# Sigmoid attention and a gated FFN on one core: two pairs of gate and value columns of the first group as block products

## The chip, the cores and the metric

One Trainium2 chip, of which the kernel uses one core. The time is the device time of one execution in microseconds; the figure for a kernel is the median of its runs. The engines of the core are PE (TensorE, matrix products), DVE (VectorE), ACT (ScalarE), POOL (GpSimd) and SP (SyncE, here only a queue that issues DMAs). Each runs its own instructions in the order in which the program lists them, and waits on semaphores for the others.

## The reference

```python
# q, k, v: (8, 12, 448, 64); w_gate, w_val: (768, 1536); w_out: (1536, 768); all float32
scores = scale * np.matmul(q, k.transpose(0, 1, 3, 2)) - np.log(S)      # scale = 1/sqrt(64), S = 448
attn = 1.0 / (1.0 + np.exp(-scores))                                    # a sigmoid, no softmax
attn_out = np.matmul(attn, v)
x = attn_out.transpose(0, 2, 1, 3).reshape(8 * 448, 12 * 64)            # 3584 tokens of 768
gate = np.maximum(x @ w_gate, 0.0)
val = x @ w_val
return gate * val @ w_out                                               # (3584, 768)
```

So eight batches each go through attention, and their 448 tokens each through a gated FFN whose weights are the same for all.

## The kernel before

The engine order is written out by hand (`tc.manual_schedule()`, L73): what the Python code calls first, each engine does first. Buffers come from pools; an instruction that writes a buffer waits until the earlier readers of it are done.

**Attention.** Twelve heads form six pairs, and two pairs make one of three head groups g. A unit (`qk_unit`, L294) is one key chunk c of seven for one g: 16 small matmuls in fours give the scores, two banks of PSUM, and two sigmoids on ACT write `PT`. When all seven chunks of a g are there, `pv_group` does 28 matmuls and DVE scales the two results into `xT` (L184). Each batch b has 21 units, cut into five or six steps m by the list `cuts`. k and q must be transposed first. For batches 0 and 1, PE does it (`pe_transposes`). From batch 2 on, DVE copies rows into `rel` (L215) and SP issues a DMA that transposes them into `qkT` (`dma_transposes`, L211).

**FFN, two ways.** Two batches make a group of 896 tokens. Plain (`gv`, L328): for one f of twelve (128 gate columns and the same value columns) six matmuls for the gate and six for the value; ACT takes the positive part, DVE multiplies into `hT`. In blocks (`gv_units`, L503): gate and value together, of both batches of a group, are a two by two block product which is done with seven products in place of eight (Strassen's scheme in Winograd's form). It needs sums of weights (`gate_sums`, `unit_sums`) and sums of `xT` blocks (`batch_sums`, which overwrites one block of `xT` in place), and it adds up with copies on ACT and DVE. One such unit does two f: seven products for each, three matmuls of 448 columns to a product. It uses six banks `b`, `a`, `c` (two each), and the seventh product adds into `b`, after DVE has read `b` in `plus` (L530). The down projection is done in the same way for pairs of 128-token tiles (`down_pair`, L429): seven products of six matmuls of 384 columns, with sums of `hT` blocks (`token_sums`, `more_token_sums`) and sums of `wo` (`weight_sums` 0 to 3, L397, once in the kernel, which need both halves of `wo`). Tile number 3 of an odd group takes the last 128 tokens of the group before it, which lie in `aside`.

**Which way where.** Group 0 (batches 0 and 1) goes the plain way for all twelve f, in `gv_queue`: each step of batches 1, 2 and 3 takes `mix[m]` of them from the queue after its units, and `hooks[m]` puts other work between them. Batch 0 is done in two halves of the queries (256 and 192 columns), so each f gives two entries for it and one for batch 1. Groups 1 to 3 go the block way: steps with `mix[m]` of 0 call `next_work`, which takes one entry of `work`: a pair of f, or a down pair. `jobs` run inside such an entry after its second product (`beside`), `behind` after its last.

**Loads.** All inputs and weights go through POOL's queue (`load`, `load_v`, `load_gv`, `load_o`), in the program's order and with fp32 turned to fp16 on the way. `hold` (L646) is a tiny copy on POOL that reads a transposed `qkT`; what stands behind it on POOL is issued only when that transpose has landed. The twelve f of `wg` and `wv` are all loaded before the last inputs of batch 1. `load_v(2)` follows `hold(2, 1)` at the end of batch 1 (L653). k, q and v of batch 3 follow in the first step of batch 2 (L759). `load_o(0)` and `load_o(1)` follow `hold(3, 1)` and `hold(3, 2)` in the fourth and sixth step of batch 2 (L716 to L718).

**Weight sums in batch 3.** `weight_sums(0)` is a hook of step 1, 1 and 2 one of step 2, and 3 a job of step 3, which is the first down pair.

Of the kernel before, what the change touches and what calls it, by code (L numbers as in the profile page):

```python
# [17 lines left out]
def kernel(  # L18
# [19 lines left out]
    NFC = DF // P  # L38
    TW = 2 * NCH
    QCUT = 4  # L40
    HALVES = ((0, QCUT), (QCUT, NCH))

    qk_scale = 1.0 / math.sqrt(D)
# [8 lines left out]
    relp = ctx.enter_context(tc.tile_pool(name="relp", bufs=2))  # L52
    qkTp = ctx.enter_context(tc.tile_pool(name="qkTp", bufs=3))
    PTp = ctx.enter_context(tc.tile_pool(name="PTp", bufs=11))
    xTp = ctx.enter_context(tc.tile_pool(name="xTp", bufs=3))
    hTp = ctx.enter_context(tc.tile_pool(name="hTp", bufs=1))
    ysbp = ctx.enter_context(tc.tile_pool(name="ysbp", bufs=4))
    gsbp = ctx.enter_context(tc.tile_pool(name="gsbp", bufs=6))
    first_sbuf = ExitStack()
    early = first_sbuf.enter_context(tc.tile_pool(name="early", bufs=1))  # L60
# [92 lines left out]
    load_gv(2, 4)  # L153
    load_gv(4, 6)
    load(1, 0, 1, "kq")
    load_gv(6, 9)
    load(1, 1, 2, "kq")
    load_gv(9, 12)
    load_v(1)
    load(1, 2, 3, "kq")  # L160

# [250 lines left out]
        sub(S2, S1, A11)  # L412
        sums["y"] = S1, S2, S4

    def more_token_sums(g, p):
        A11, A12, A21, A22 = token_blocks(g, p)
        S1, S2, S4 = sums["y"]
        sub(S4, A12, S2)
        sub(A21, A11, A21)

    def scaled(o, ps):
        nc.vector.tensor_scalar(
# [67 lines left out]
        lo, hi = slice(*ks), slice(HD + ks[0], HD + ks[1])  # L490
        return [late["X"][:, i, lo] for i in range(3)] + [x1[:, lo], x1[:, hi], x2[:, lo], x2[:, hi]]

    def batch_sums_t1(g):
        T1, _, _, B11, _, B12, _ = batch_blocks(g, (0, HD))
        sub(T1, B12, B11)

    def batch_sums(g, ks):
        T1, T2, T4, _, B21, B12, B22 = batch_blocks(g, ks)
        sub(T2, B22, T1)
        sub(B12, B22, B12)  # L500
        sub(T4, B21, T2)

    def gv_units(g, fs, beside, first_copy, then, split):  # L503
        x1, x2 = xT_tiles[2 * g], xT_tiles[2 * g + 1]
        T1, T2, T4 = (late["X"][:, i] for i in range(3))
        B11, B21, T3, B22 = x1[:, 0:HD], x1[:, HD:NDC], x2[:, 0:HD], x2[:, HD:NDC]
        b, a, c = ([bank(nm) for _ in fs] for nm in ("u", "g1", "g2"))
        later((4, 5, 6, 7, 2, 3))
        gs = [[gsbp.tile([P, S], FP32, tag="gsb", name="gsb") for _ in range(3)] for _ in fs]
        sets = []  # L510
        for u, f in enumerate(fs):
            us, cols = slice(u * P, (u + 1) * P), slice(f * P, (f + 1) * P)
            S1, S2, S4 = (t[:, :, us] for t in sums["w"])
            sets.append((
                wg[:, 0:HD, cols], wg[:, HD:NDC, cols], wv[:, HD:NDC, cols],
                S1, S2, wv[:, 0:HD, cols], S4,
            ))
        del sums["w"]

        def product(ps, i, W, first=True):  # L520
            for u in range(len(fs)):
                products([(ps[u], S, HD, sets[u][i], W, first)])

        def copy(i, ps, by=nc.scalar.copy):
            for u in range(len(fs)):
                by(gs[u][i][:], ps[u][:, 0:S])  # L526

        def plus(i, ps):
            for u in range(len(fs)):
                nc.vector.tensor_tensor(  # L530
                    out=gs[u][i][:], in0=ps[u][:, 0:S], in1=gs[u][i][:], op=AOP.add
                )

        product(b, 0, B11)
        copy(0, b, first_copy)
        product(a, 1, B21)
        beside()
        plus(0, a)
        product(b, 4, T2, False)
        copy(1, b)  # L540
        product(c, 3, T1)
        copy(2, c)
        product(b, 5, T3, False)
        plus(2, b)
        product(c, 6, B22, False)
        plus(1, c)
        product(b, 2, T4, False)

        def finish(even):
            for u in range(len(fs)):  # L550
                if even:
                    gated(g, fs[u], 0, S, gs[u][0], b[u])
                else:
                    gated(g, fs[u], S, S, gs[u][1], gs[u][2])

        if split:
            finish(False)
            then()
            finish(True)
        else:  # L560
            finish(True)
            finish(False)
            then()

    gv_queue = deque()

# [61 lines left out]
                after[(i, u)]()  # L628
    slots[5].pv()
    push_first(1, range(0, 6))  # L630
    for f0 in range(6, 12, 2):
        for half in range(2):
            push_first(half, range(f0, f0 + 2))

# [3 lines left out]
    def pv_finish(b):  # L638
        pv_group(b, NG - 1)
        if b < 2:  # L640
            push_gv(b, 0, S, range(NFC))

    first_psum.close()
    open_banks("ring1")
# [8 lines left out]
    def late_loads():  # L653
        dma_transposes(2, 1)
        hold(2, 1)
        load_v(2)


    work = deque()

    def push_group(g):
        if g > 0:
            work.extend([("w", g, (f, f + 1)) for f in range(0, NFC, 2)])
        work.extend([("y", g, p) for p in ((3, 0, 1, 2) if g % 2 else (0, 1, 2))])

    def prepare():
        if work:
# [6 lines left out]
    def next_work(jobs=(), behind=(), alone=False):  # L674
        kind, g, i = work.popleft()

        def run(jobs):
            for job in jobs:
                job()

        if kind == "y":
            down_pair(
                g, i, lambda: (more_token_sums(g, i), run(jobs)),
                lambda: (run(behind), prepare()), not work, scaled_act if alone else scaled,
            )
        else:
            first_copy = nc.scalar.copy if alone else nc.vector.tensor_copy
            if work[0][0] == "w":
                gv_units(g, i, lambda: (prepare(), run(jobs)), first_copy, lambda: run(behind), False)
            else:  # L690
                gv_units(
                    g, i, lambda: run(jobs), first_copy, lambda: (run(behind), prepare()), alone
                )

    ffn_mix(1, [(1, lambda: both(1, 0))])
    for b in range(1, B):
# [6 lines left out]
        count = len(cuts) - 1  # L703
        hooks = {}
        if b == 1:
            mix = (3, 3, 3, 3, 3, 2)
            hooks = {
                1: [(1, lambda: both(1, 1))],
                3: [(1, lambda: both(1, 2))],
                4: [(3, lambda: dma_transposes(2, 0))],  # L710
                5: [(2, late_loads)],
            }
        elif b == 2:
            mix = (2, 2, 1, 1, 2, 1)
            hooks = {
                3: [(0, lambda: (dma_transposes(3, 0), dma_transposes(3, 1), hold(3, 1), load_o(0)))],  # L716
                5: [
                    (1, lambda: (dma_transposes(3, 2), hold(3, 2), load_o(1))),  # L718
                    (0, lambda: (gate_sums(0, 2), gate_sums(2, 4))),
                ],  # L720
            }
            open_late()
        elif b == 3:
            mix = (1, 1, 1, 0, 0)
            hooks = {
                0: [(0, lambda: (gate_sums(4, 6), gate_sums(6, 8)))],
                1: [(0, lambda: weight_sums(0))],
                2: [(0, lambda: (prepare(), weight_sums(1), weight_sums(2)))],
            }
        else:  # L730
            mix = (0,) * count
        for m in range(count):
            jobs, behind = [], []
            for i, (g, c) in enumerate(order[cuts[m] : cuts[m + 1]]):
                if m in pv_at and i == pv_at[m][1]:
                    if m == 0:
                        pv_finish(b - 1)
                        if b == 2:
                            push_group(0)
                    else:  # L740
                        pv_group(b, pv_at[m][0])
                qk_unit(b, g, c)
            if m == 0 and b > 1 and b != 3:
                jobs.append(lambda: dma_transposes(b, 2))
            if b == 3 and m == count - 2:
                jobs.append(lambda: weight_sums(3))
            elif b == 4 and m == 2:
                jobs.append(lambda: (gate_sums(8, 10), gate_sums(10, 12)))
            elif b == 3 and m == count - 1:
                jobs.append(lambda: (dma_transposes(4, 0), dma_transposes(4, 1)))  # L750
            elif 0 <= m - count + 2 and 3 < b < B - 1:
                jobs.append(lambda: dma_transposes(b + 1, m - count + 2))
            if b == 1:
                if m == 0:
                    load(2, 0, 1, "kq")
                    load(2, 1, 2, "kq")
                    load(2, 2, 3, "kq")
            elif m == 0 and b + 1 < B:
                jobs.append(lambda: (load(b + 1, 0, 3, "kq"), load_v(b + 1)))  # L759
            if b % 2 and b > 2:  # L760
                if m == count - 1:
                    push_group(b // 2)
                    (jobs if b == B - 1 else behind).append(
                        lambda: (batch_sums_t1(b // 2), batch_sums(b // 2, (0, 1)))
                    )
                    if b == B - 1:
                        jobs.append(lambda: pv_finish(b))
                        behind.append(lambda: batch_sums(b // 2, (1, HD)))
            elif b > 3 and m == 0:
                behind.append(lambda: batch_sums(b // 2 - 1, (1, HD)))  # L770
            if mix[m]:
                for job in jobs:
                    job()
# [35 lines left out]
```

## Time and profile before

| | |
|---|---|
| runs | 404.38, 405.57, 405.37, 405.56, 404.32 us |
| median | 405.37 us |
| the profiled execution | 404.38 us, span of its instructions 402.6 us |
| mean granted PE clock | 0.993 |

The span runs from the first to the last instruction. Busy times of the engines overlap, so they don't add up to it. Where PE has a gap, what matters is what it waited for, and then why that was late. Two granted clocks below 1 show in the record: one stretch of 3.4 us between 113.99 and 117.40 us at half speed, and one at the very end.

| stage of the first half | from | to |
|---|---|---|
| batch 1, six steps | 33.84 | 62.98 |
| batch 2, six steps | 62.98 | 92.90 |
| batch 3, steps 0 to 2 | 92.90 | 105.81 |
| batch 3, step 3 (first down pair) | 105.81 | 119.78 |
| batch 3, step 4 (second down pair) | 119.78 | 130.94 |

These are the starts of the score matmuls in PE's timeline.

### The profile page before, as it was taken

The page shows a single profiled execution, that of the slowest core. Times are in us where ns is not written, and L with a number is a line of the kernel's source. Part 1 is how long each engine was busy: PE and PEld are TensorE (multiplying, and loading weights), DVE is VectorE, ACT ScalarE, POOL GpSimd, SP SyncE. Part 2 cuts the span into 40 slices and gives each one's busy share as a digit, 9 for nine tenths or more (in the row PEclk, how much of TensorE's full clock was granted, in tenths as well). Part 3 has the DMA queues.
Part 4 walks back from the last instruction along what each step waited for, and adds up shares of the span by engine and source line. Part 5 has one row for each costly group of instructions (what it writes and reads, how often), then busy time and mean ns, then how long its engine had stood idle before and what let it go on. Part 6 is the DMA issues. An engine that isn't in the chain of part 4 may idle for free.

```text
span 402.6 us, 8701 instructions
## 1 busy us (share of the span) xinstructions
PE 389.0 (97%) x3476; PEld 217.2 (54%) x3476; DVE 280.1 (70%) x570; ACT 230.0 (57%) x482; POOL 49.3 (12%) x74
## 2 busy tenths in 40 slices
PE   8999999999888999999999999999999999999995
PEld 3678775544444554554555555455455555555562
DVE  2453435344577799999766889999785699897661
ACT  5946777779815565655656565565545544433221
POOL 8643302301400300003000030000000000000000
PEclk9999999999989999999999999999999999999999
DMA  9999995998997794235916598012203220000235
GB/s 149 195 199 205 204 149 93 184 182 151 173 168 140 152 213 73 46 47 63 186 41 166 126 148 183 16 32 47 47 2 80 80 78 2 0 1 2 78 99 138
DMA packets 67257, 43.69 MB, mean 109 GB/s; under 512 B 35856, under 2 KB 63760, under 8 KB 67216
## 3 DMA queue, kind: packets, MB, share of 16 engines
q0 software_dynamic: 29200, 23.33, 37.9%
q1 hardware_dynamic: 37584, 19.24, 22.8%
q10 hardware_dynamic: 432, 0.56, 0.5%
q8 instruction: 27, 0.44, 0.4%
q14 instruction: 14, 0.11, 0.1%
HBM read 47.19 MB, written 11.01 MB: 145 GB/s over the span
## 4 chain that ended last, share of the span: by engine, by line
PE 86%; DMA 6%; DVE 3%; ACT 3%; issue 1%; ACTq 0%; POOL 0%; POOLq 0%
PE u L384 33%; PE g L384 15%; PE y L384 9%; PE qk_ps L232 7%; PE pv_ps L250 6%; PE g_ps L333 6%; PE v_ps L333 6%; DMA qkT<-rel 3%; DMA wo<-in_moe_w_out_dram 2%; ACT PT L187 2%; PE warm_ps L175 1%; PE trt L201 1%; DVE hT L319 1%; DVE xT L184 1%; ACT ysb L427 1%
## 5 line engine op out<-in xcount | busy, mean ns | idle before, releaser
L187 ACT ACTIVATE PT<-qk_ps 128x448 f16<-128x448 f32 (+3 forms) x318 | 150.8, 591 | 55.5 <-PE qk_ps L232 55.2
L384 PEld LDWEIGHTS <-S 128*128 128x128 f16 x576 | 56.4, 98 | 49.9 <-issue 4.7
L232 PE MATMUL qk_ps<-qkT 64*64 64x448 f16 (+2 forms) x756 | 50.2, 336 | 2.3 <-DMA qkT<-rel 1.5
L427 ACT ACTIVATE ysb<-u 128x384 f32<-128x384 f32 x32 | 15.7, 491 | 58.4 <-PE u L384 58.2
L526 ACT COPY gsb<-u 128x448 f32<-128x448 f32 x48 | 25.6, 533 | 31.8 <-PE u L384 30.5
L384 PEld LDWEIGHTS <-hT 128*128 128x128 f16 x312 | 30.0, 99 | 24.2 <-issue 3.1
L530 DVE TENSOR_TENSOR gsb<-g,gsb 128x448 f32<-128x448 f32 x72 | 41.5, 617 | 0.1
L319 DVE SCALAR_TENSOR_TENSOR hT<-gate_sb,v_ps 128x256 f16<-128x256 f32 (+2 forms) x36 | 14.6, 421 | 37.4 <-ACT gate_sb L342 21.1
L250 PE MATMUL pv_ps<-PT,v 64*64 64x448 f16 (+2 forms) x756 | 37.2, 329 | 0.7 <-issue 0.7
L184 DVE TENSOR_SCALAR xT<-pv_ps 128x448 f16<-128x448 f32 (+2 forms) x53 | 27.8, 566 | 14.1 <-PE pv_ps L250 13.5
L232 PEld LDWEIGHTS <-qkT 64*64 64x64 f16 x756 | 20.2, 105 | 26.9 <-issue 15.8
L333 PE MATMUL g_ps<-xT,wg 128*128 128x256 f16 (+2 forms) x216 | 33.5, 291 | 0.1
L333 PE MATMUL v_ps<-xT,wv 128*128 128x256 f16 (+2 forms) x216 | 33.3, 290 | 0.0
L384 PEld LDWEIGHTS <-wv 128*128 128x128 f16 x216 | 21.1, 98 | 19.7
L384 PEld LDWEIGHTS <-wg 128*128 128x128 f16 x216 | 20.3, 98 | 20.6 <-issue 3.0
L384 PE MATMUL u<-wo,hT 128*128 128x384 f16 x156 | 30.3, 331 | 0.1
L530 DVE TENSOR_TENSOR gsb<-u,gsb 128x448 f32<-128x448 f32 x36 | 21.4, 624 | 12.6 <-PE u L384 12.5
L250 PEld LDWEIGHTS <-v 64*64 64x64 f16 x756 | 22.0, 107 | 11.7 <-issue 1.6
L110 POOL DMA_DIRECT2D k<-in_k_dram x14 | 10.9, 779 | 126.3 <-DVE rel L215 119.2
L333 PEld LDWEIGHTS <-wg 128*128 128x128 f16 x216 | 18.5, 98 | 11.5 <-issue 5.0
L333 PEld LDWEIGHTS <-wv 128*128 128x128 f16 x216 | 20.2, 98 | 7.4
L444 DVE SCALAR_TENSOR_TENSOR ysb<-u,ysb 128x384 f32<-128x384 f32 x14 | 7.8, 558 | 23.3 <-ACT ysb L427 13.9
(71 smaller groups left out, 539.7 us busy)
## 6 DMA issues: line engine op xcount, KB each, us to landing
out_dram<-ysb SPq DMA_DIRECT2D x53, 192.0 KB, 2.9
k<-in_k_dram POOLq DMA_DIRECT2D x5, 672.0 KB, 10.8
q<-in_q_dram POOLq DMA_DIRECT2D x5, 672.0 KB, 14.4
v<-in_v_dram POOLq DMA_DIRECT2D x8, 336.0 KB, 14.6
v<-in_v_dram POOLq DMA_DIRECT2D x16, 168.0 KB, 14.2
wo<-in_moe_w_out_dram POOLq DMA_DIRECT2D x2, 1152.0 KB, 10.4
k<-in_k_dram POOLq DMA_DIRECT2D x8, 224.0 KB, 10.4
q<-in_q_dram POOLq DMA_DIRECT2D x6, 224.0 KB, 11.3
```

What stands on the lines that cost most here:

```text
L110: nc.gpsimd.dma_start(t16[:, xs, cs], rows_of(src, b)[:, xs, cs])
L184: nc.vector.tensor_scalar(out=xT, in0=src, scalar1=XSCALE, scalar2=None, op0=AOP.mult)
L187: nc.scalar.activation(PT_ap, ps_ap, AF.Sigmoid, bias=sig_bias, scale=qk_scale)
L232: nc.tensor.matmul(out_of(hh)[o : o + 64, :], qkT[rows, c, cols], qkT[rows, NCH + c0 : NCH + c1, cols], start=True, stop=True, tile_positi ...
L250: nc.tensor.matmul(ps[hh][64 * r : 64 * r + 64, 0:qn], v16[rows, 2 * g + hh, c * D : (c + 1) * D], pieces[c][rows, hh, :], start=(c == 0), ...
L319: nc.vector.scalar_tensor_tensor(out=dst[:, f, a - d : z - d], in0=gate_sb[:, a - o : z - o], scalar=0.0, in1=val[:, a - o : z - o], op0=relu,
L333: nc.tensor.matmul(ps[-1][:, 0:qn], wt[:, dc, f * P : (f + 1) * P], xT_tiles[b][:, dc, q0 : q0 + qn], start=(dc == 0), stop=(dc == NDC - 1),)
L384: nc.tensor.matmul(ps[:, 0:n], A[:, k_, :], W[:, k_, :], start=(first and k_ == 0), stop=(k_ == kn - 1), skip_group_check=True,)
L427: nc.scalar.activation(o, ps[:, 0:HM], AF.Copy, scale=OUT_SCALE)
L444: nc.vector.scalar_tensor_tensor(out=o, in0=ps[:, 0:HM], scalar=OUT_SCALE, in1=o, op0=AOP.mult, op1=AOP.add)
L526: by(gs[u][i][:], ps[u][:, 0:S])
L530: nc.vector.tensor_tensor(out=gs[u][i][:], in0=ps[u][:, 0:S], in1=gs[u][i][:], op=AOP.add)
```

## The change

Group 0 now does only the f 0 to 7 the plain way; f 8 to 11 become two block units in steps 1 and 2 of batch 3. Their weights are loaded behind batch 2's inputs (8, 9 after `hold(2, 1)`, and 10, 11 behind k and q of batch 3), `load_v(2)` moves ahead, and batch 3's `v` and both halves of `wo` stand one behind the other after `hold(3, 1)`. Since `xT` of batches 0 and 1 is now needed until batch 3, there are four buffers of it, and three of `ysb`.

With that the hooks are dealt out anew: `batch_sums` for group 0 (one sum to a step), `gate_sums` in another order, `weight_sums` 0 in step 1, 1 in step 2, 2 and 3 in step 3. `mix` is smaller in batches 1 to 3. `dma_transposes(4, 0)` stands ahead of the units of batch 3's last step. In the last unit of a group, the second half of the gating (`finish(False)`) is put off (`pending`) into the next down pair, between its sums. Group 1 takes its down pairs in the order 0, 3, 1, 2, where it was 3, 0, 1, 2.

```diff
+    NPLAIN = 8
-    xTp = ctx.enter_context(tc.tile_pool(name="xTp", bufs=3))
+    xTp = ctx.enter_context(tc.tile_pool(name="xTp", bufs=4))
-    ysbp = ctx.enter_context(tc.tile_pool(name="ysbp", bufs=4))
+    ysbp = ctx.enter_context(tc.tile_pool(name="ysbp", bufs=3))
...
     load(1, 0, 1, "kq")
-    load_gv(6, 9)
+    load_gv(6, NPLAIN)
     load(1, 1, 2, "kq")
-    load_gv(9, 12)
     load_v(1)
...
-    def more_token_sums(g, p):
+    def more_token_sums(g, p, between):
         A11, A12, A21, A22 = token_blocks(g, p)
         S1, S2, S4 = sums["y"]
+        sub(A21, A11, A21)
+        between()
         sub(S4, A12, S2)
-        sub(A21, A11, A21)
...
+    def batch_sums(g, which, ks=(0, HD)):
+        T1, T2, T4, B11, B21, B12, B22 = batch_blocks(g, ks)
+        for i in which:
+            sub(*((T1, B12, B11), (T2, B22, T1), (B12, B22, B12), (T4, B21, T2))[i])
...
         else:
             finish(True)
-            finish(False)
             then()
+            return lambda: finish(False)
...
-    for f0 in range(6, 12, 2):
+    for f0 in range(6, NPLAIN, 2):
...
-            push_gv(b, 0, S, range(NFC))
+            push_gv(b, 0, S, range(NPLAIN))
...
     def late_loads():
         dma_transposes(2, 1)
         hold(2, 1)
-        load_v(2)
+        load_gv(8, 10)
...
     def push_group(g):
-        if g > 0:
-            work.extend([("w", g, (f, f + 1)) for f in range(0, NFC, 2)])
-        work.extend([("y", g, p) for p in ((3, 0, 1, 2) if g % 2 else (0, 1, 2))])
+        work.extend([("w", g, (f, f + 1)) for f in range(0 if g else NPLAIN, NFC, 2)])
+        tiles = (0, 1, 2) if g % 2 == 0 else (3, 0, 1, 2) if g == B // 2 - 1 else (0, 3, 1, 2)
+        work.extend([("y", g, p) for p in tiles])
...
+        def run_pending():
+            while pending:
+                pending.pop()()
+
         if kind == "y":
             down_pair(
-                g, i, lambda: (more_token_sums(g, i), run(jobs)),
+                g, i, lambda: (more_token_sums(g, i, run_pending), run(jobs)),
...
+            last = work[0][0] != "w"
+            rest = gv_units(
+                g, i, lambda: (run_pending(), last or prepare(), run(jobs)),
+                nc.scalar.copy if alone else nc.vector.tensor_copy,
+                lambda: (last and prepare(), run(behind)), alone and last,
+            )
+            if rest:
+                if last:
+                    pending.append(rest)
+                else:
+                    rest()
...
         if b == 1:
-            mix = (3, 3, 3, 3, 3, 2)
+            mix = (2, 1, 2, 1, 2, 1)
...
         elif b == 2:
-            mix = (2, 2, 1, 1, 2, 1)
+            mix = (2, 1, 1, 1, 1, 1)
             hooks = {
-                3: [(0, lambda: (dma_transposes(3, 0), dma_transposes(3, 1), hold(3, 1), load_o(0)))],
+                1: [(0, lambda: batch_sums(0, (0,)))],
+                2: [(0, lambda: batch_sums(0, (1,)))],
+                3: [(0, lambda: (
+                    dma_transposes(3, 0), dma_transposes(3, 1), hold(3, 1), load_v(3),
+                    load_o(0), load_o(1),
+                ))],
+                4: [(0, lambda: (batch_sums(0, (3,)), gate_sums(0, 2), gate_sums(8, 10)))],
                 5: [
-                    (1, lambda: (dma_transposes(3, 2), hold(3, 2), load_o(1))),
-                    (0, lambda: (gate_sums(0, 2), gate_sums(2, 4))),
+                    (1, lambda: dma_transposes(3, 2)),
+                    (0, lambda: (gate_sums(2, 4), gate_sums(10, 12))),
                 ],
             }
         elif b == 3:
-            mix = (1, 1, 1, 0, 0)
+            mix = (1, 0, 0, 0, 0)
             hooks = {
-                0: [(0, lambda: (gate_sums(4, 6), gate_sums(6, 8)))],
-                1: [(0, lambda: weight_sums(0))],
-                2: [(0, lambda: (prepare(), weight_sums(1), weight_sums(2)))],
+                0: [(0, lambda: (batch_sums(0, (2,)), prepare(), gate_sums(4, 6)))],
             }
...
+            if b == 3 and m == count - 1:
+                dma_transposes(4, 0)
...
-            if b == 3 and m == count - 2:
-                jobs.append(lambda: weight_sums(3))
-            elif b == 4 and m == 2:
-                jobs.append(lambda: (gate_sums(8, 10), gate_sums(10, 12)))
-            elif b == 3 and m == count - 1:
-                jobs.append(lambda: (dma_transposes(4, 0), dma_transposes(4, 1)))
+            if b == 3 and m:
+                jobs.append((
+                    None,
+                    lambda: weight_sums(0),
+                    lambda: weight_sums(1),
+                    lambda: (weight_sums(2), weight_sums(3)),
+                    lambda: dma_transposes(4, 1),
+                )[m])
+            elif b == 4 and m == 1:
+                jobs.append(lambda: gate_sums(6, 8))
...
                     load(2, 2, 3, "kq")
+                    load_v(2)
             elif m == 0 and b + 1 < B:
-                jobs.append(lambda: (load(b + 1, 0, 3, "kq"), load_v(b + 1)))
+                jobs.append(lambda: load(b + 1, 0, 3, "kq"))
+                jobs.append(lambda: load_gv(10, 12) if b == 2 else load_v(b + 1))
```

More of the change, by code (lines that the diff above doesn't have):

```diff
@@ L491, in batch_blocks @@
         return [late["X"][:, i, lo] for i in range(3)] + [x1[:, lo], x1[:, hi], x2[:, lo], x2[:, hi]]
[L493 to L501, printed above, removed]
+    def batch_sums(g, which, ks=(0, HD)):
+        T1, T2, T4, B11, B21, B12, B22 = batch_blocks(g, ks)
+        for i in which:
+            sub(*((T1, B12, B11), (T2, B22, T1), (B12, B22, B12), (T4, B21, T2))[i])
     def gv_units(g, fs, beside, first_copy, then, split):
@@ L655, in late_loads @@
         hold(2, 1)
-        load_v(2)
+        load_gv(8, 10)
     work = deque()
+    pending = []
     def push_group(g):
-        if g > 0:
-            work.extend([("w", g, (f, f + 1)) for f in range(0, NFC, 2)])
-        work.extend([("y", g, p) for p in ((3, 0, 1, 2) if g % 2 else (0, 1, 2))])
+        work.extend([("w", g, (f, f + 1)) for f in range(0 if g else NPLAIN, NFC, 2)])
+        tiles = (0, 1, 2) if g % 2 == 0 else (3, 0, 1, 2) if g == B // 2 - 1 else (0, 3, 1, 2)
+        work.extend([("y", g, p) for p in tiles])
     def prepare():
@@ L686, in next_work @@
         else:
[L687 to L693, printed above, removed]
+            last = work[0][0] != "w"
[9 more added lines that the diff above has]
+                    rest()
     ffn_mix(1, [(1, lambda: both(1, 0))])
@@ L763 @@
                     (jobs if b == B - 1 else behind).append(
-                        lambda: (batch_sums_t1(b // 2), batch_sums(b // 2, (0, 1)))
+                        lambda: (batch_sums(b // 2, (0,)), batch_sums(b // 2, (1, 2, 3), (0, 1)))
                     )
@@ L767 @@
                         jobs.append(lambda: pv_finish(b))
-                        behind.append(lambda: batch_sums(b // 2, (1, HD)))
+                        behind.append(lambda: batch_sums(b // 2, (1, 2, 3), (1, HD)))
             elif b > 3 and m == 0:
-                behind.append(lambda: batch_sums(b // 2 - 1, (1, HD)))
+                behind.append(lambda: batch_sums(b // 2 - 1, (1, 2, 3), (1, HD)))
             if mix[m]:
```

## The prediction

> **What bounds the kernel now.** I read the page first, then busy time by stage, then PE's waits, then the order of time around them.
>
> ```profile
> span 402.6 us, 8701 instructions
> ...
> PE 389.0 (97%) x3476; PEld 217.2 (54%) x3476; DVE 280.1 (70%) x570; ACT 230.0 (57%) x482; POOL 49.3 (12%) x74
> ...
> PEclk9999999999989999999999999999999999999999
> ```
>
> TensorE is the bound: 389.0 of 402.6 us. What is left lies mostly in two places: some 5 us at the end, and the stages of batch 3. Here are batch 1, batch 2 and the last two steps of batch 3 (start:end, length, then busy time of each engine, granted clock, DMA share, GB/s):
>
> ```profile
> 33.80:63.00 29.20, 29.14 (x406) 23.01 (x404) 11.33 (x29) 23.50 (x60) 5.77 (x9) 1.00 1.09 167
> 63.00:92.90 29.90, 29.90 (x277) 14.78 (x277) 11.87 (x32) 22.81 (x52) 6.92 (x11) 1.00 0.94 157
> ...
> 105.80:119.80 14.00, 10.21 (x63) 4.93 (x62) 8.92 (x14) 4.71 (x11) 0.00 (x0) 0.88 1.16 192
> 119.80:130.90 11.10, 9.69 (x91) 5.46 (x90) 7.89 (x19) 6.33 (x14) 0.00 (x0) 1.00 0.66 131
> ```
>
> Batches 1 and 2 run PE without a gap. The step that does the first down pair takes 14.0 us and PE is busy for 10.2 of it, at a granted clock of 0.88. PE's waits between 100 and 200 us name the causes:
>
> ```profile
> PE u L384 <- DVE ysb L422: 2.0, 1, 2.0
> PE y L384 <- DMA wo<-in_moe_w_out_dram: 1.8, 1, 1.8
> PE qk_ps L232 <- DMA qkT<-rel: 1.5, 1, 1.5
> ```
>
> The timeline shows where they come from (start, duration, engine, line, operation, and in brackets the idle time before it):
>
> ```profile
> 91.25 0.18 POOL L647 COPY gate<-qkT 1x2 f16<-1x2 f16 x1 [16.73 <-DMA qkT<-rel]
> 91.70 0.87 POOL L164 DMA_DIRECT2D wo<-in_moe_w_out_dram  x1 [0.27 <-issue]
> 99.82 0.18 POOL L647 COPY gate<-qkT 1x2 f16<-1x2 f16 x1 [7.26 <-DMA qkT<-rel]
> ```
>
> ```profile
> 103.15 1.36 DVE L375 TENSOR_TENSOR T<-wo 128x2304 f16<-128x2304 f16 x1 [0.43 <-DMA wo<-in_moe_w_out_dram]
> ...
> 109.99 1.36 DVE L375 TENSOR_TENSOR T<-wo,T 128x2304 f16<-128x2304 f16 x1 [2.25 <-DMA wo<-in_moe_w_out_dram]
> 110.01 1.15 PE L384 MATMUL y<-wo,hT 128*128 128x384 f16 x6 [1.82 <-DMA wo<-in_moe_w_out_dram]
> ...
> 113.14 1.29 PE L384 MATMUL u<-T,S 128*128 128x384 f16 x6 [1.98 <-DVE ysb L422]
> ```
>
> Each half of `wo` is issued only after a copy on POOL has seen a transposed `qkT` land. The halves land 11.4 and 9.4 us after their issue. DVE stands at the weight sum until then, and the copy of the first result (L422) is queued behind it.
>
> **The change, part by part.** (1) PE work. Four values of f leave the plain products. One plain f costs six-matmul groups of 0.655 us twice (256 columns), 0.495 twice (192) and 1.14 twice (448): 4.58, four make 18.3. The two block units bring 84 matmuls of 448 columns, 14 groups of 1.137: 15.9. Gain 2.4.
>
> (2) The old stalls. The step at 105.81 lasted 13.97; 16 score matmuls (0.97) and seven products of 0.98 make 7.85, so 6.1 was stall and slow clock. The next lasted 11.16 against 9.4 (with a `pv` of 1.32): 1.8. Both causes move: `wo` is now needed in `weight_sums(0)` one unit into batch 3, and the rows for `qkT` of batch 4 are copied ahead of the last step's scores, some 4 us sooner, which removes the 1.5 us wait. I take both sums out, 7.9, and price below what takes their place.
>
> (3) The new order of the tail of a group's last unit (`pending`) and of the down pairs lets L422's copy precede two products of 0.6 us. PE now loses 0.4 us at the first down pair of groups 1 and 2 (201.99 + 0.98 against 203.37, and the same at 298.41): gain 0.8.
>
> (4) Batch 1 loses four f of the first batch, 9.2 us of PE, and falls from 29.1 to 19.9. ACT does not shrink alike: 42 sigmoids at a pitch of 0.453 are 19.0, nine relus of 0.28 are 2.5, so 21.5. ACT becomes the bound there. PE may run ahead by the banks it has, so the loss lies between 0 and 3; the `pv` of batch 1's last group cannot start before its last sigmoid, which gives 1.4. I take 1.4.
>
> (5) Inputs. Weights of f 8 to 11 no longer stand ahead of batch 2's inputs: 1152 KB at 205 GB/s (75 to 80 us) are 5.8 us, with the smaller third load 7.7 us in all. PE comes 9.2 us sooner less 1.4, so those inputs keep their lead; cost nothing, and up to 1.5 us if the lead is gone. But `load_gv(8, 10)`, 768 KB, now goes ahead of batch 3's k and q, behind the same POOL copy. Batch 2's fourth step, whose end copies batch 3's rows (84.20 now), comes at 84.2 - 9.2 - 2.3 (one plain f of batch 1 less by then) + 1.4 = 74.1; call it T. q landed 11.5 us after its issue; issued near 64.1 it lands at 75.7, against 74.4 where DVE reads it. DVE waits 1.3; behind it are `xT` copies of 1.15 that hold two banks for the step after the next. PE: 0.6, bounds 0 and 1.7.
>
> (6) `wo`. POOL's copy passed 7.05 us after DVE's first row copy (91.25 - 84.20); with the wait T + 8.4. New in front of `wo` stand batch 3's three `v` loads, 672 KB, 3.4 us. The two measured landings give 0.45 + 3.4 + 9.4 = 13.2 to 0.45 + 3.4 + 11.4 = 15.3 after that copy; nearer the clean one, since only one transpose shares the rings: 13.5, so T + 21.9 = 96.0. Who waits: DVE reaches `weight_sums(0)` 3.5 us into the first block unit, near T + 16.4, and stands there 5.5 us. Queued behind it are the two sums that free bank `a` and the two that free bank `b` (L530, 0.6 each); PE's seventh product needs `b`. It could start 6.8 us into the unit, T + 19.7; it gets `b` 1.36 + 1.75 after `wo` lands, T + 25.0. PE stall 5.3; part of that is DVE's own lag, since three hooks now stand ahead of the unit's first copy, so I take 5.0. Bounds: if the `v` loads cost nothing and the rows do not wait, `wo` lands as now, 18.9 us after the row copy, and the stall is 2.4; with 15.3 it is 7. The second half of `wo` follows 5.8 later, ahead of its reader. Only the first wait counts.
>
> (7) Clock. Between 110 and 120 us the rows show 0.90 and 0.76, 1.7 us of clock lost after gaps of 1.8 and 2.0. I charge the same 1.7 for one gap of 5; bounds 0 and 2.6.
>
> The Trainium skill, "TensorE: Matmul & The Clock Gate", Part 1, speaks against this change: it has the clock halved after an idle window of about 3.4 us and restored only after a busy one, so a gap of 5 us can hit two windows where the gaps here hit one. By that rule term (7) could be 3.4 and the sum 1.7 higher; no row here has so long a gap.
>
> (8) DVE in batch 3. The block units bring copies, sums and gated pairs where a plain f has 0.77 us of DVE. In the unit steps DVE has some 10 us of work against 9 to 10 of PE. In the first down pair, the two deferred gated pairs (1.5) and two weight sums (1.27 each by start to start) stand before the third term: its fifth product waits 1.3, its seventh 0.3, together 1.6; a bank held by the last gated pair costs 0.5. I take 2.1, bounds 1 and 3.5.
>
> (9) Three `ysb` buffers: a pair's second tile now waits for the store of the pair before. In the tail that store is issued at 376.88, lands by 380.18, and the write comes at 381.22. Hidden by 1.0 us; a store as slow as the 4.1 us seen at 384.9 would still cost nothing there, since that one is the other tile. A fourth `xT` buffer frees only.
>
> Sum: -2.4 - 7.9 - 0.8 + 1.4 + 0.6 + 5.0 + 1.7 + 2.1 = -0.3. Span 402.3; with the 1.8 us around it (404.38 against 402.60) 404.1. The profiled execution is 1.0 below the median of five, 405.37; the runs stand at 404.3 and at 405.4 to 405.6.
>
> **Rivals.** Wait short (B): the transposes are done sooner and `wo` lands as early as now relative to the row copy, stall 2.4, clock 0.9, 404.1 - 3.4 = 400.7; without (4) 399.3. For it: the first half of `wo` shared the rings with a transpose that took 8.3 us to land, against 4.1 for the fastest, and need not do so again. Against: 672 KB more are ahead of it. Slower (C): `wo` lands 15.3 after POOL's copy, stall 7, clock 2.6, and DVE's lag is at its upper bound: +2.0 + 0.9 + 1.4 = 408.4. It decides against the change from a `wo` landing about 2 us later than I take. For it: DVE has no slack left in batch 3. Against: DVE has slack in batch 2 (11.9 of 29.9). No effect (D): the blocks' 2.4 and the old stall are traded for the same stall one unit earlier, 405.4.
>
> **How the numbers follow.** A measurement of this kernel tells 0.2%, 0.8 us, from no change; faster means under 404.6, slower over 406.2. My forecast (A), 404.1, own range 402.0 to 406.2: 0.45, of which 0.25 faster, 0.15 the same, 0.05 slower. B 0.25, faster. C 0.24, slower. D 0.06, half of it the same and half slower. Faster 0.50, same 0.18, slower 0.32. The range, 399.5 to 408.0, holds A, D, most of B and half of C.
>
> **What would show it.** In the changed profile: PE in batch 1 with gaps that sigmoids end (4); DVE idle before the first T sum by DMA `wo`, 3 to 6 us, and PE's longest wait in the seventh product of the first block unit (6); a stretch of clock 0.5 right after (7); PE waits of 1 to 2 us in the first down pair (8); none on `ysb`. If DVE does not wait for `wo`, I am wrong by 5 to 7 us; if the clock falls twice, by 2 the other way.

## The result, and the profile after

| | before | after |
|---|---|---|
| median of all runs | 405.57 us (79 runs) | 407.35 us (42 runs) |
| the profiled execution | 404.38 us, span 402.6 us | 406.03 us, span 404.3 us |
| ratio after to before | | 1.0046 [1.0036, 1.0056] |

The changed kernel is slower by 0.46%, where the prediction had 404.1 us and faster as the likeliest. The head of the page of after:

```profile
span 404.3 us, 8607 instructions
...
PE 388.0 (96%) x3416; PEld 212.1 (52%) x3416; DVE 293.9 (73%) x592; ACT 229.3 (57%) x478; POOL 50.9 (13%) x75
...
PEclk9999999999899999999999999999999999999999
```

TensorE has 1.0 us less to do and the span is 1.7 us longer, so 2.7 us more of gaps. DVE has 13.8 us more. Busy time by stage of after (start:end, length, busy time of each engine, granted clock, DMA share, GB/s): batch 1, batch 2, the first block unit's step, the first down pair's step, and the stretch at half clock:

```profile
34.35:56.22 21.87, 21.59 (x307) 15.25 (x306) 8.58 (x21) 20.09 (x50) 6.32 (x9) 1.00 1.11 176
56.22:82.44 26.22, 25.66 (x255) 12.40 (x254) 13.11 (x31) 22.79 (x52) 5.16 (x7) 1.00 1.12 173
87.02:103.70 16.68, 10.70 (x60) 4.70 (x60) 11.05 (x20) 5.73 (x12) 4.89 (x7) 0.91 1.15 196
...
114.15:123.71 9.56, 8.35 (x59) 4.41 (x58) 9.07 (x18) 4.58 (x10) 0.00 (x0) 1.00 0.00 1
```

```profile
100.72:104.13 3.41, 2.76 (x14) 0.94 (x17) 3.04 (x7) 0.00 (x0) 0.00 (x0) 0.50 1.20 206
```

Batch 1 and batch 2 shrank as meant, and the first down pair fell from 13.97 to 9.56 us. The unit's step (the third row) takes 16.68 us, and PE works for 10.70 of it. PE's waits over the whole span say why:

```profile
PE u L384 <- DVE gsb L526: 5.4, 1, 5.4
...
PE u L384 <- DVE wo L375: 1.1, 1, 1.1
PE u L384 <- DVE gsb L522: 0.5, 1, 0.5
```

The waits that stood here before (2.0 for L422, 1.8 for `wo`, 1.5 for `qkT`) are gone; one of 5.4 took their place. The timeline of after, engine by engine, shows its making: POOL's issues, then DVE, then PE (start, duration, operation, and in brackets the idle time before it).

```profile
84.07 0.21 POOL L643 COPY gate<-qkT 1x2 f16<-1x2 f16 x1 [18.25 <-DMA qkT<-rel]
84.58 0.75 POOL L115 DMA_DIRECT2D v<-in_v_dram  x1 [0.30 <-PE qk_ps L232]
85.32 1.26 POOL L117 DMA_DIRECT2D v<-in_v_dram  x2
86.57 1.69 POOL L164 DMA_DIRECT2D wo<-in_moe_w_out_dram  x2
```

```profile
92.69 0.55 DVE L375 TENSOR_TENSOR S<-wg,S 128x768 f16<-128x768 f16 x1
98.36 1.36 DVE L375 TENSOR_TENSOR T<-wo 128x2304 f16<-128x2304 f16 x1 [5.12 <-DMA wo<-in_moe_w_out_dram]
99.64 1.15 DVE L526 TENSOR_TENSOR gsb<-g,gsb 128x448 f32<-128x448 f32 x2
100.70 1.15 DVE L526 TENSOR_TENSOR gsb<-u,gsb 128x448 f32<-128x448 f32 x2
```

```profile
94.64 1.30 PE L384 MATMUL g<-xT,S 128*128 128x448 f16 x6
101.37 2.40 PE L384 MATMUL u<-X,wv 128*128 128x448 f16 x6 [5.43 <-DVE gsb L526]
```

POOL issues `v` of batch 3 and then both halves of `wo`. The first half lands 11.8 us after its issue at 86.57. DVE was ready for it at 93.24 and stands until 98.36 at the first of the weight sums; behind it are the four sums of L526, the last two of which read the bank that PE's seventh product adds into. That product (101.37) starts 5.4 us late, and right after the gap it takes 2.40 us where 1.30 is usual, at a clock of 0.50.

### The profile page after: what moved, and what is told of

It is laid out like the page before. It is cut to its first block, busy times and chain, and to the rows that moved or that the text cites. A ratio compares the mean times of both kernels' runs of the same rounds, so it can differ in the third digit from the quotient of the medians.

```text
span 404.3 us, 8607 instructions
## 1 busy us (share of the span) xinstructions
PE 388.0 (96%) x3416; PEld 212.1 (52%) x3416; DVE 293.9 (73%) x592; ACT 229.3 (57%) x478; POOL 50.9 (13%) x75
## 4 chain that ended last, share of the span: by engine, by line
PE 84%; DMA 6%; ACT 3%; POOL 3%; DVE 2%; issue 1%; ACTq 0%; DVEq 0%; POOLq 0%
PE u L384 36%; PE g L384 16%; PE y L384 9%; PE pv_ps L250 8%; PE qk_ps L232 7%; PE g_ps L333 4%; PE v_ps L333 3%; DMA wo<-in_moe_w_out_dram 3%; DMA wv<-in_moe_w_val_dram 3%; ACT PT L187 2%; POOL q L111 1%; PE trt L201 1%; POOL v L117 1%; POOL k L111 1%; DVE hT L319 1%
## 5 line engine op out<-in xcount | busy, mean ns | idle before, releaser
L384 PEld LDWEIGHTS <-S 128*128 128x128 f16 x612 | 59.7, 98 | 50.4 <-issue 1.3
L522 ACT COPY gsb<-u 128x448 f32<-128x448 f32 x52 | 27.7, 533 | 34.0 <-PE u L384 32.6
L526 DVE TENSOR_TENSOR gsb<-g,gsb 128x448 f32<-128x448 f32 x80 | 46.1, 617 | 0.1
L384 PEld LDWEIGHTS <-wv 128*128 128x128 f16 x240 | 23.7, 99 | 28.1 <-issue 6.6
L384 PEld LDWEIGHTS <-wg 128*128 128x128 f16 x240 | 22.5, 98 | 23.0 <-issue 3.6
L526 DVE TENSOR_TENSOR gsb<-u,gsb 128x448 f32<-128x448 f32 x40 | 23.7, 623 | 14.4 <-PE u L384 14.4
L384 PE MATMUL u<-X,wv 128*128 128x448 f16 x120 | 27.1, 363 | 5.4 <-DVE gsb L526 5.4
L250 PEld LDWEIGHTS <-v 64*64 64x64 f16 x756 | 22.0, 107 | 12.5 <-issue 2.6
L319 DVE SCALAR_TENSOR_TENSOR hT<-gate_sb,v_ps 128x256 f16<-128x256 f32 (+2 forms) x24 | 9.8, 420 | 24.2 <-ACT gate_sb L342 10.1
L384 PE MATMUL u<-X,S 128*128 128x448 f16 x120 | 26.0, 352 | 0.5 <-DVE gsb L522 0.5
L384 PE MATMUL u<-xT,wg 128*128 128x448 f16 x120 | 26.1, 353 | 0.1
L384 PE MATMUL g<-X,S 128*128 128x448 f16 x120 | 26.0, 352 | 0.0
L384 PE MATMUL u<-xT,wv 128*128 128x448 f16 x120 | 26.0, 352 | 0.0
## 6 DMA issues: line engine op xcount, KB each, us to landing
v<-in_v_dram POOLq DMA_DIRECT2D x16, 168.0 KB, 12.5
```

Of the source, the lines that this page charges most:

```text
L250: nc.tensor.matmul(ps[hh][64 * r : 64 * r + 64, 0:qn], v16[rows, 2 * g + hh, c * D : (c + 1) * D], pieces[c][rows, hh, :], start=(c == 0), ...
L319: nc.vector.scalar_tensor_tensor(out=dst[:, f, a - d : z - d], in0=gate_sb[:, a - o : z - o], scalar=0.0, in1=val[:, a - o : z - o], op0=relu,
L384: nc.tensor.matmul(ps[:, 0:n], A[:, k_, :], W[:, k_, :], start=(first and k_ == 0), stop=(k_ == kn - 1), skip_group_check=True,)
L526: nc.vector.tensor_tensor(out=gs[u][i][:], in0=ps[u][:, 0:S], in1=gs[u][i][:], op=AOP.add)
```

## The experiments

**Theory A.** DVE stands in order at `weight_sums(0)`; move the sum, or the load, or DVE's arrival, and PE's gap moves by as much. **Rivals:** the loss lies in batch 1, where ACT now sets the pace; in the clock; in the deferred gating; or the block units simply cost what they save. All ratios are to the kernel before, run on the same chip. The edits are shown in short, some of them in words; the marks - and + still say what went and what came.

**1. The weight sums one step later**, the loads untouched:

```diff
-    step 1's jobs: weight_sums(0);  step 2's jobs: weight_sums(1)
+    step 2's jobs: weight_sums(0);  behind step 2's unit: weight_sums(1)
```

> The changed kernel with the first sum of wo halves (T1) moved out of the first block unit into the second, and the second sum (T2) behind the second unit's last product. Theory A (the loss is DVE standing at T1 until the first half of wo lands, with the sums that free PE's banks queued behind it, and the slow clock that follows the gap): the 5.4 us gap ahead of the first unit's seventh product is gone, so is the stretch of half clock after it, some 1 us comes back in the first down pair; about 6 us under the changed kernel, ratio to the kernel before 0.990 (0.985 to 0.995). Theory B (DVE simply has more work than PE in batch 3, the wait only hides that): DVE still runs late, at most 2 us gained, ratio 1.000 to 1.004.

399.61 us, 0.9843 [0.9817, 0.9869]. Stages of this kernel, the first unit and the first down pair, and its PE waits:

```profile
86.68:96.67 9.99, 9.44 (x60) 4.50 (x60) 9.71 (x19) 5.73 (x12) 4.93 (x7) 1.00 1.16 185
...
106.92:117.30 10.38, 8.52 (x59) 4.41 (x58) 10.26 (x19) 4.58 (x10) 0.00 (x0) 1.00 0.71 115
```

```profile
PE u L384 <- DVE wo L375: 1.3, 1, 1.3
...
PE u L384 <- DVE gsb L522: 0.5, 1, 0.5
```

The 5.4 us wait and the half-clock stretch are gone; the unit's step falls by 6.7 us, and the down pair, whose sums come later, gives 0.8 of that back. It takes back all of after's loss of 1.8 us and some 6 more. That is more than the 6 us expected (the ratio lies just under the range given); the two profiled spans differ by 6.5 us, and after's median lies 1.3 above its profiled execution, where this kernel's lies 0.1 above.

**2. The first half of `wo` ahead of `v`**, the sums untouched:

```diff
-    hold(3, 1), load_v(3), load_o(0), load_o(1)
+    hold(3, 1), load_o(0), load_v(3), load_o(1)
```

> The changed kernel with the first half of wo issued ahead of batch 3's v, the second half behind it. Theory A: the first half lands 3.4 us sooner, the gap shrinks from 5.4 to about 2 us and the clock falls less often; 3.4 to 5 us under the changed kernel, ratio 0.993 to 0.997. Theory B: ratio as the changed kernel's, 1.002 to 1.005.

402.85 us, 0.9928 [0.9901, 0.9954]. The weight sum on DVE, and PE's wait:

```profile
94.99 1.36 DVE L375 TENSOR_TENSOR T<-wo 128x2304 f16<-128x2304 f16 x1 [2.06 <-DMA wo<-in_moe_w_out_dram]
```

```profile
PE u L384 <- DVE gsb L526: 2.4, 1, 2.4
```

`wo` lands 3.4 us sooner, and the gap falls by 3.0. The gap follows the landing. The clock still falls to half for one stretch of 3.41 us, from 97.95 on.

**3. The positive part of batch 1's plain products on DVE** in place of ACT, for all f but the first of the second batch's first six:

```diff
-    push_first(1, range(0, 6))
+    push_first(1, range(0, 1))
+    push_first(1, range(1, 6), False)
...
-            push_first(half, range(f0, f0 + 2))
+            push_first(half, range(f0, f0 + 2), False)
```

> The changed kernel with the gate's positive part in batch 1's nine plain entries taken on DVE instead of ACT (2.5 us less on ACT there). Theory C (batch 1 is bound by ACT, 21.9 us against 19.9 of PE work): batch 1 falls by 1.5 to 2 us, ratio 1.0046 goes to about 1.001. If the later wait for wo sets the time of batch 3 whatever comes before it, the wait grows by as much and nothing is gained: ratio 1.0046. Theory A in its plain form says gained, since the loads of wo start from a DVE copy that comes sooner too.

405.42 us, 0.9995 [0.9979, 1.0010]. Batch 1 takes 20.48 us in place of 21.87, so ACT did set its pace. But the gap grew, and the clock fell for twice as long (PE's wait, DVE's, then the stretch):

```profile
PE u L384 <- DVE gsb L526: 6.2, 1, 6.2
```

```profile
97.43 1.36 DVE L375 TENSOR_TENSOR T<-wo 128x2304 f16<-128x2304 f16 x1 [5.83 <-DMA wo<-in_moe_w_out_dram]
```

```profile
96.76:103.59 6.83, 3.15 (x18) 1.14 (x21) 5.79 (x10) 0.18 (x1) 0.00 (x0) 0.50 1.19 208
```

By these two profiles two thirds of the 1.4 us won in batch 1 are lost again by the start of batch 4 (132.61 against 133.35, with batch 1 started 0.25 sooner): DVE comes 1.6 us sooner to a load that lands 0.9 sooner. The load too was issued 1.6 us sooner, but took 12.5 us to land in place of 11.8. The profiled execution of after had one window of half clock, though, where this one has two. By the ratios the kernel is 0.5% or 2.0 us faster than after, so ACT's pace was worth between 0.5 and 2.0 us.

**4. No deferred gating**, the old order of the sums and of the down pairs:

```diff
-    finish(True); then(); return lambda: finish(False)
+    finish(True); finish(False); then()
```

> The changed kernel with the order at the end of a group's units as before: no second half of the gating put off into the next down pair, the sums of the down pair in the old order, group 1's down pairs 3, 0, 1, 2. My term of 0.8 us for this order: 0.8 us slower than the changed kernel, ratio 1.0066. Rival (the deferred products only lengthen the first down pair, where PE waits 1.1 us for a weight sum): up to 1 us faster than the changed kernel, ratio 1.002.

407.37 us, 1.0055 [1.0030, 1.0079]: times do not tell it from after, but the interval holds the 1.0066 expected and not the rival's 1.002. The profile does tell it: batch 5 takes 46.57 us in place of 46.17, which is the 0.4 us a transition that the prediction had read off. From the start of batch 4 to the end it takes 271.6 us, as the kernel before does (271.7), where after takes 270.9 and the nine other profiles with the new order take 270.5 to 271.0. And a wait appears that after does not have:

```profile
PE u L384 <- DVE ysb L423: 0.8, 3, 0.3
```

**5. Experiments 1 and 3 together.**

> Both edits at once: the wo sums later (as in the first experiment) and batch 1's positive part on DVE. The DVE-only run gained 1.3 us in batch 1 by its trace (34.10 to 54.58 against 34.35 to 56.22) and lost 0.8 of it in a longer wait for wo. Theory: with the wait gone the batch 1 gain is kept, 1.3 us under the first experiment, ratio 0.981 (0.978 to 0.984). Rival: batches 2 and 3 wait for loads that do not come sooner (k and q of batch 3, v of batch 3), the gain is lost there: ratio 0.984 as the first experiment.

398.35 us, 0.9837 [0.9811, 0.9863], and 398.71, 0.9832 [0.9798, 0.9866], when it ran a second time beside the experiments 9 to 11:

> The combination once more (later sums, positive part on DVE), unchanged, for a second interval beside the others of this call: ratio 0.981 to 0.986.

From the start of batch 1 to that of batch 4 it takes 91.65 us (34.34 to 125.99), where it was 92.83 with the sums alone (34.11 to 126.94): with the load out of the way, 1.2 of the 1.4 us won in batch 1 stay won. By its median this is the fastest kernel of the study, though its interval overlaps that of experiment 1.

**6. All of it:** 1, 2 and 3, with the four sums spread, one to a unit or behind it.

```diff
+    behind step 1: weight_sums(0); step 2: (1); behind step 2: (2); step 3: (3)
```

> The first half of wo ahead of v, the four sums of wo dealt out one to a place where PE does not wait for them (behind the first unit, in the second, behind the second, in the first down pair), and the positive part on DVE. Theory: the first down pair, 10.4 us in the first experiment against 7.85 of PE work, comes to some 8.5: 1.5 us under the combination of two, ratio 0.977 (0.973 to 0.981). Rival: DVE's total in batch 3 is the limit, the sums only move the wait: ratio 0.980 to 0.984.

399.39 us, 0.9855 [0.9835, 0.9876], well short of what was expected. The down pair's step did fall, from 10.38 to 9.74 us, but the step before it grew from 10.25 to 11.82. DVE there:

```profile
103.07 1.36 DVE L375 TENSOR_TENSOR T<-wo,T 128x2304 f16<-128x2304 f16 x1 [1.83 <-DMA wo<-in_moe_w_out_dram]
```

The second sum now comes ahead of the second half of `wo`, and `pv` waits 0.8 us for the `v` that was put behind the first half. The wait only moved.

**7. One pair of f in blocks, not two** (`NPLAIN = 10`), on top of experiment 1, with the loads, sums and `mix` for it.

> The first experiment with one pair (f 10 and 11) as block products, not two; f 8 and 9 go the plain way in batches 1 to 3 and their weights are loaded early again. By my terms a pair saves PE 1.2 us, and batch 1 gets back 4.6 us of PE work where ACT is the bound by 2 us: 1.2 - 1.0, so within 0.5 us of the first experiment, ratio 0.984 to 0.986. Rival 1: the pair gives its full 1.2 or more: 0.987 to 0.989. Rival 2: the block units cost more in DVE waits than they save: below 0.983.

399.46 us, 0.9859 [0.9839, 0.9878], against 0.9843 in experiment 1, with intervals that overlap. Batch 4 starts at 126.91 against 126.94, but batch 1 had started 0.56 us sooner, so over these three batches one pair takes 0.5 us more than two. The second pair brings 0 to 0.6 us of the 1.2 that its products save. That ACT's pace in batch 1 takes the rest is argued and not shown.

**8. The kernel before, with both halves of `wo` after the first hold:**

```diff
-    hold(3, 1), load_o(0)        ...   hold(3, 2), load_o(1)
+    hold(3, 1), load_o(0), load_o(1)
```

> The kernel before with both halves of wo issued one behind the other after the first POOL copy (no second copy). Its first down pair lost 6.1 us, of which the wait for the second half 1.8, the copy behind the sums 2.0 and half clock 1.7. The second half should land near 108.5 in place of 109.96: 1 to 1.5 us, and perhaps one stretch of half clock less: ratio 0.992 to 0.998. Rival: the row copies' transposes of the third head group then wait behind wo and PE stalls there: ratio over 1.000.

402.61 us, 0.9938 [0.9909, 0.9967]. The first down pair takes 12.1 us in place of 13.97: two fifths of what after gains in that step comes from the loads' order alone.

**9. The gap filled:** 28 matmuls into banks that nothing reads, between the sixth and the seventh product of the first unit of after.

```diff
+        for i in range(28):
+            nc.tensor.matmul(ps[i % 2][:, 0:S], wg[:, 0, 0:P], x1[:, 0, :], start=True, stop=True)
         product(b, 2, T4, False)
```

> The changed kernel with 28 matmuls of 448 columns (5.2 us, results unused) put into the 5.4 us gap ahead of the first unit's seventh product. They cost nothing if they end before the bank comes free; DVE and the loads stand as they were. Theory: the clock stays at 1.0 in batch 3, the seventh product and what follows run at full speed; 1.7 us less in an execution with one stretch of half clock, 3.4 in one with two (most executions of the changed kernel, by their mean clock of 0.988 to 0.990): ratio 0.997 to 1.000. Rival: the clock costs nothing because DVE and the loads set the pace after the gap: ratio 1.004 to 1.006.

406.31 us, 1.0033 [1.0007, 1.0059]. Its first two unit steps, PE in them, and DVE at the first weight sum:

```profile
86.79:103.12 16.33, 14.89 (x87) 7.21 (x86) 10.20 (x19) 5.73 (x12) 4.87 (x7) 1.00 1.16 199
103.12:114.42 11.30, 11.00 (x87) 5.52 (x87) 9.92 (x19) 5.83 (x12) 0.00 (x0) 1.00 1.07 173
```

```profile
95.54 5.46 PE L546 MATMUL warm_ps<-xT,wg 128*128 128x448 f16 x28
101.90 1.30 PE L384 MATMUL u<-X,wv 128*128 128x448 f16 x6 [0.90 <-DVE gsb L526]
...
104.55 1.51 PE L250 MATMUL pv_ps<-PT,v 64*64 64x448 f16 x26 [0.15 <-DVE hT L319]
```

```profile
98.89 1.36 DVE L375 TENSOR_TENSOR T<-wo 128x2304 f16<-128x2304 f16 x1 [5.89 <-DMA wo<-in_moe_w_out_dram]
```

The clock stays at 1.00, and the seventh product takes 1.30 us in place of 2.40. But the next step grows to 11.30 from 10.45, since `pv` cannot go on before DVE's gated pairs, which come when they came (104.3 in after, 104.55 here). Batch 4 starts at 133.62, against 133.35. `wo` landed 0.5 us later in this execution (98.89 against 98.36), so it is fairer to count from there: to the start of batch 4 it is 34.73 us at full clock, 34.99 with one stretch of half clock (after) and 35.18 with two (experiment 3). The clock was worth 1.0 us by the medians and 0.5 by the ratios, whose intervals overlap: near the rival's figure, that it cost nothing, and below the theory's.

**10. In experiment 5, the third weight sum behind the first of the late token sums** (`more_token_sums`), ahead of the deferred gating:

```diff
-    step 3's jobs: weight_sums(2), weight_sums(3)
+    pending.append(weight_sums(2));  step 3's jobs: weight_sums(3)
```

> The combination of later sums and the positive part on DVE, with the third sum of wo (in place) ahead of the deferred gating in the first down pair. Theory: PE's wait of 1.3 us for it goes, 0.6 to 0.9 us under the combination, ratio 0.981 to 0.983. Rival: the wait moves to the next product (its sum of hT blocks is later now): no change, 0.983 to 0.985.

398.68 us, 0.9829 [0.9796, 0.9862], no different from 5. The down pair's step is 10.38 us in both; PE's wait is 1.0 for a copy of L445 where it was 1.3 for the weight sum.

**11. No block units at all:** the kernel before, with the first half of `wo` in the place of batch 3's `v`, `v` and the second half behind the first hold, and the early transposes of batch 4.

```diff
-    batch 2, first step: k, q, v of batch 3;  hold(3, 1), load_o(0);  hold(3, 2), load_o(1)
+    batch 2, first step: k, q of batch 3, load_o(0);  hold(3, 1), load_v(3), load_o(1)
+    batch 3, last step: dma_transposes(4, 0) ahead of its units
```

> The kernel before, all of group 0 plain, with the first half of wo in the place of batch 3's v among the loads of batch 2, v and the second half behind the POOL copy, and the first transpose of batch 4 ahead of the last step's scores. What the block units are worth by themselves. Theory: nearly all of the old stall goes (wo's second half lands near 106.5), 4.5 to 6 us under the kernel before, ratio 0.985 to 0.989, 1 to 2 us above the combination. Rival: a plain group without the stall is as fast as the blocks or faster, ratio under 0.983. Other rival: the first transposes of batch 3 wait behind the larger load and PE stalls: over 0.990.

399.19 us, 0.9844 [0.9807, 0.9881], just under the 0.985 to 0.989 expected, and not under the rival's 0.983. Its first down pair takes 9.95 us, with one long wait left:

```profile
111.31 1.14 PE L384 MATMUL u<-T,S 128*128 128x384 f16 x6 [1.63 <-DVE ysb L422]
```

So 6 us are to be had without a single block unit, and the best kernel with two of them is 0.5 to 0.8 us ahead of it by the medians, inside the intervals. Nor is that lead the units' alone: from the start of batch 4 on, experiment 5 takes 271.0 and 270.8 us and this kernel 271.6, and it lacks the new order of gating and down pairs (experiment 4).

## Why the prediction was wrong

The mechanism was the one that was forecast, in its place, though some 2 us later (`wo` landed at 98.36, where 96.0 was forecast): `wo` late for `weight_sums(0)`, DVE standing there, the seventh product short of bank `b`. Experiments 1 and 2 show it from two sides, by moving the reader and the load. What failed is the sum: gains and losses of some 11 us each were set against one another, and the total came out 2 us above the -0.3 that the text ended with. The terms that were too small are (6), the stall for `wo`, by 1.0 us, and (4), ACT in batch 1, by 0.6; another 0.5 us stood under no term. Of the rivals, D (the old stall traded for one a unit earlier) was nearest in kind, and put at 405.4 it too was short.

| step | predicted | read from the profile of after |
|---|---|---|
| (2) old stalls and (8) DVE in batch 3 | -7.9 + 2.1 | -5.9: the two down pairs' steps, 25.13 to 19.20 |
| (3) later groups | -0.8 | -0.8: from batch 4's start to the end, 271.7 to 270.9 |
| (4) ACT in batch 1 | +1.4 | +2.0: 21.87 against 19.9 of PE work |
| (5) inputs in batch 2 | +0.6 | +0.8: 26.22 against 25.4 |
| (6) stall for `wo` | +5.0 | +6.0: 5.43, and 0.55 for the first copy (L522) |
| (7) clock | +1.7 | +1.4: 2.76 us of PE work at half speed |
| no term | | +0.5: batch 1 starts at 34.35, not 33.84 |

With (1) at -2.4, which no single row shows, the right column gives +1.6; the spans differ by 1.7.

(1) Of the 2.4 us of PE work to be saved, the page shows 1.0 (389.0 to 388.0). Little of it reaches the end: experiment 7 finds 0 to 0.6 us for the second pair, and 11, with none, comes within 0.5 to 0.8 us of the best.

(2) and (8) were right together to 0.1 us; of the waits in (8) one is listed, 1.1 us where the fifth product was to wait 1.3. But (2) booked the whole cure of the old stalls to the change, and experiments 8 and 11 show that the order of the loads, with no block unit, brings it (in 11 together with the earlier transposes): the units then add the new wait. That was the reading to be had from the trace before: what heals the stalls and what makes the new one are separate edits.

(4) is 0.6 too small. The text put the ACT bound of batch 1 at 21.5 us and then took only the delay of the last `pv`; the stage did take ACT's time, 21.87, and experiment 3 shows it to be ACT's, since taking the work off it gives 1.4 back. (5) DVE waited 0.8 us for `q`, not 1.3, and batch 2 still lost 0.8.

(6) is the largest mis-sized term, 1.0 us too small, and the working itself had 5.3 before it was cut to 5.0 for DVE's lag. That lag showed in its own place, as the 0.55 us for L522, and had to be added, not taken off. Counted from POOL's copy at 84.07, `wo` landed after 14.3 us, between the 13.5 taken and the 15.3 of rival C; DVE stood ready after 9.2, where 8.0 was forecast. So DVE's own wait was 5.1 us, where 5.5 was forecast.

(7) The clock fell once in the profiled execution, for 3.41 us. PE had 2.76 us of work in that stretch, so the size is 1.4 and not 1.7, and the reason is weaker than thought: experiment 9, which keeps the clock up, gains 1.0 us at most, as what follows the gap goes at DVE's pace. The Trainium skill, "TensorE: Matmul & The Clock Gate", Part 1, halves the clock after an idle window of some 3.4 us until a busy one. The lengths here fit: 3.41 us in after and 6.83 in experiment 3, one window and two. The idle window need not be empty, though: the 3.41 us ahead of the stretch hold 1.08 us of PE work in experiment 2, whose gap is 2.4 us, and 1.43 in the kernel before, whose gaps are 1.8 and 2.0. By the page's penalty of half the throttled time (its Terms) experiment 3 would lose 3.4 us, an estimate. The rows show PE busy for only 3.15 of those 6.83 us, as it stood in the gap for the rest.

(9) held: no wait on `ysb` in after that the buffers would cause.

The 0.5 us at the start of batch 1 is no larger than what the profiles differ by among themselves: the ten profiles of this study with the same first loads start it between 33.57 and 34.59, and three with before's between 33.83 and 34.32.

One step lay outside the terms. The sum, -0.3 us, was made on the profiled execution (404.38) and then judged against a median 1.0 higher, so that no change at all read as faster. Both kernels' profiled executions lie 1.2 to 1.3 us below their medians. On one base the forecast was 404.1 to 404.38, a ratio of 0.999, and by the prediction's own bound that is no change.

What stays open: what the half-clock stretches cost the kernel before, some of whose runs had none and took 402.0 to 402.7 us, while at a mean clock of 0.988 to 0.990 they took 404 to 407; the gaps may differ between those runs, so this is no measurement of the clock. And what block units are worth here: 5 and 11 lie within each other's intervals.

## What to carry to other kernels

When an edit moves the first reader of a load forward, look at what stands behind that reader on its own engine: an engine that works in order turns a late load into a late bank, and moving the reader back by one unit was worth more (407.35 to 399.61 us) than moving the load ahead (402.85). Split a change into the edits that heal and the edits that save, and price each alone; here the order of the loads, with the earlier transposes, did 6 us without a block unit, and the best kernel with units was at most 0.8 us ahead of that. And where a sum of large terms ends near zero, judge it on the base that it was made on, and let the sign stay open.

## What the hardware showed

A gap of 5.4 us in PE's work was followed by one half-clock stretch of 3.41 us in one execution, and gaps of 6.2 and 5.5 us by 6.83 us, two of them (experiments 3 and 4). A gap of 2.4 us was enough for one (experiment 2). Of the 43 executions of after, the profiled one among them, 35 had a mean clock of 0.986 to 0.990, four 0.992 and four 0.996. The median of the last four is 406.65 us, that of the 35 is 407.42, so what lowers the mean further, a second stretch if the profiles of experiments 3 and 4 are a guide, costs 0.8 us and not another 1.7. (The mean clock also counts a stretch at the very end, which differs from run to run, so it does not give the number of stretches by itself.) Filling the gap with matmuls that nobody needs kept the clock at 1.00 and left the time where it was, to within 1.0 us.
